# Attention and two feed-forward blocks on one core: queries in two buffers, a first load in two parts, the gate's row on another queue, and a new order of attention's steps

## The chip, the cores and the metric

The kernel runs on one core of one Trainium2 chip. The metric is the time of one execution on the device, in microseconds (us). The engines are TensorE (PE: matmuls, and PEld: the weight loads for them), VectorE (DVE), ScalarE (ACT), GpSimd (POOL) and SyncE (SP, which here only issues DMAs). Each engine works through its own queue in order, and waits on semaphores for the others.

## The reference

Attention is computed for 4 batches of 8 heads, 576 tokens and 64 columns a head: a causal softmax and, beside it, a read from a memory matrix, mixed by a gate for each head. Two feed-forward blocks follow on all 2304 tokens.

```python
scores = q @ k.T / 8;  causal mask;  a = softmax(scores)
local = a @ v
q_p = where(q > 0, q, exp(q) - 1) + 1
mem_out = (q_p @ M_prev) / (q_p . z_prev + 1e-6)
g = 1 / (1 + exp(-beta))                      # one for each head
x = g * mem_out + (1 - g) * local             # then to (2304, 512)
h = x @ w_in;  x = max(0.01 * h, h) @ w_out   # 512 -> 2048 -> 512
out = ((x @ w_a) * (x @ w_b)) @ w_o2          # 512 -> 1536 -> 512
```

## The kernel before

Attention works on 16 pairs of heads, w = 0 to 15. For a pair, `load_qk` brings keys and queries with the head's columns on partitions into one of three buffers (`raw0` to `raw2`). `scores` multiplies them on PE in row tiles of 128 tokens, tile i being (i + 1) * 128 columns wide (the causal part); `scores_tail` does the last 64 rows of two pairs at once. `least` (line 566, or 596 for the tail) is a DVE instruction that adds the mask, writes the scores to SBUF and takes their extreme; `exp_of` (line 513) is the exponential on ACT with its sum; `recip` (lines 524 and 528, DVE) inverts the sums; `norm` (line 540, on DVE or POOL) multiplies a row tile by its inverse sum and by 1 - gate. These instructions are 128, 256, 384, 512 or (tail) 576 columns wide, one for each head and row tile: 144 `norm` steps in all. `probs_T` transposes the result on PE (line 617) and ACT or DVE copies it out of PSUM (lines 331, 333); `pv_local` (line 696) and `pv_memory` (line 668) are the matmuls with v and with the memory, and `store` copies their sum out.

Beside that, two pairs at a time share a load of 128 x 1536 queries (`load_quad`, u = 0 to 7, 768 KB, tile `qraw`), from which `phi` makes q_p: `low` (line 433, a clamp), `exp` (436, ACT), `high` (439), `times` (444 and 449: q_p times z_prev, written back into `qraw`), `total` (454, a sum over the columns) and `scale` (338). There is a single `qraw` tile, so a load can start only after `total` of the load before has read it.

`gates_of_heads` loads the 8 values of beta to all partitions (tile `bt`, on SP's queue behind two larger loads), and makes `gate`, `keep` (1 - gate), `keept` and `gateq` from it in a handful of small DVE instructions.

The order of all 1206 steps, and the engine that each runs on, is written out in `ORDER`: a letter for the engine (A ACT, D DVE, E PE, G POOL, S SP) and the step's number. Each engine issues its steps in that order. A cost table inside `Plan` (`timed`) is used in the kernel only to decide how many filling matmuls (`spin`, line 308, whose result nothing reads) PE runs while it waits at the start. Behind attention, in the same order, come 48 matmuls of the first feed-forward block (`first`), and four halves of a weight block are prepared on DVE, ACT and POOL (`weight`, lines 197 to 226). Then the two feed-forward blocks run, which the change does not touch: three matmuls for each product (lines 284 to 286).

Of the kernel before, what the change touches and what calls it, by code (L numbers as in the profile page):

```python
# [11 lines left out]
F32 = mybir.dt.float32  # L12
# [9 lines left out]
P = 128  # L22
# [8 lines left out]
def chunks(pr):  # L31
# [9 lines left out]

TURN = {"row": 97.0, "full": 152.0, "col": 152.0, "quad": 152.0}
# [73 lines left out]
def attention_moe_moe2(ctx: ExitStack, tc, kqT, qn, vn, m_prev, beta, w_in, w_out, w_a, w_b, w_o2, out):  # L116
# [172 lines left out]
    def attention(att, plan):  # L289
# [66 lines left out]
        def gates_of_heads():  # L356
# [5 lines left out]
            def left(_):  # L362
                nc.vector.tensor_scalar(keep, gate, -1.0, 1.0, ALU.mult, ALU.add)
                for j, r in enumerate(rows_):
                    nc.vector.tensor_copy(keept[r], keep[r, j:H:2])
# [814 lines left out]
```

## Time and profile before

| | |
|---|---|
| median of 3 runs | 1049.55 us (1049.55 to 1050.54) |
| the profiled execution | 1049.57 us |
| its span in the trace | 1047.4 us |
| first scores of attention start | 4.66 us into the span |
| first feed-forward matmul starts | 192.57 us |
| last matmul of attention | 214.4 us |

The profile shows one execution. Its span runs from the first to the last instruction; the 2.2 us between span and time lie around it. A window of the trace gives, for each engine, the time that it was busy, PE's granted clock (1.00 is full speed, 0.5 half of it) and the load of the DMA engines. A group of instructions has its source line, engine, operation, tiles and shape, their count, busy time and mean duration, and the idle time in front of them with what ended it. The chain of waits is followed back from the last instruction: at each step to what released it.

### The profile page before, as it was taken

How to read it: one execution, taken by the hardware profiler on the slowest of the kernel's cores; microseconds unless marked ns; L12 is line 12 of the kernel's file. 1: busy time of each engine (PE TensorE's matmuls, PEld its weight loads, DVE VectorE, ACT ScalarE, POOL GpSimd, SP SyncE). 2: the span in 40 equal slices, each digit the busy share in tenths (PEclk: the TensorE clock that was granted, in tenths of full speed). 3: DMA queues.
4: the chain of work that ended last, by engine and by line, in shares of the span. 5: the costliest groups of instructions: out<-in, count | busy, mean ns of one | idle time of the engine just before them, and what ended most of it. 6: DMA issues, size and time to landing. Idle time of an engine off the chain costs nothing.

```text
span 1047.4 us, 14319 instructions
## 1 busy us (share of the span) xinstructions
PE 1031.7 (98%) x5423; PEld 830.0 (79%) x5425; DVE 714.7 (68%) x1436; ACT 391.1 (37%) x905; POOL 326.1 (31%) x273
## 2 busy tenths in 40 slices
PE   9889999999999999999999999999999999999998
PEld 4556666788888888888888887888888888888887
DVE  7889999877575757484846593772973964955324
ACT  6888888665323222222223342322112121211110
POOL 4346434025434434243434131330330420511000
PEclk9999999999999999999999999999999999999999
DMA  6233432211111111010111010110110210200022
GB/s 219 89 110 116 146 119 79 73 55 67 61 41 61 61 41 57 24 61 24 57 41 61 1 52 29 61 61 1 61 61 1 81 41 7 89 26 1 1 81 100
DMA packets 19061, 63.31 MB, mean 60 GB/s; under 512 B 2352, under 2 KB 2352, under 8 KB 18992
## 3 DMA queue, kind: packets, MB, share of 16 engines
q1 hardware_dynamic: 18992, 62.40, 17.4%
q8 instruction: 42, 0.69, 0.3%
q14 instruction: 27, 0.22, 0.1%
HBM read 57.68 MB, written 4.72 MB: 60 GB/s over the span
## 4 chain that ended last, share of the span: by engine, by line
PE 82%; DVE 12%; ACT 2%; DMA 2%; issue 1%; SPq 0%; DVEq 0%; ACTq 0%
PE b L284 26%; PE b L285 26%; PE b L286 26%; DVE p L540 3%; DVE p L566 2%; PE b L696 1%; DMA qraw<-in_qn 1%; PE b L617 1%; ACT p L513 1%; PE b L558 1%; DVE phi L439 1%; DVE xh L937 1%; DMA bt<-in_beta 1%; DVE nr L454 1%; DVE phi L433 1%
## 5 line engine op out<-in xcount | busy, mean ns | idle before, releaser
L284 PE MATMUL b<-xh,w 128*128 128x512 f32 (+1 forms) x800 | 295.2, 369 | 0.0
L285 PE MATMUL b<-xh,w 128*128 128x512 f32 (+1 forms) x800 | 294.5, 368 | 0.0
L286 PE MATMUL b<-xh,w 128*128 128x512 f32 (+1 forms) x800 | 294.3, 368 | 0.0
L223 POOL TENSOR_TENSOR wa<-wa,w 128x512 f32<-128x512 f32 x64 | 108.7, 1699 | 507.4 <-DVE wh L217 384.8
L284 PEld LDWEIGHTS b<-xh,w 128*128 128x128 f32 x800 | 150.8, 189 | 25.4
L286 PEld LDWEIGHTS b<-xh,w 128*128 128x128 f32 x800 | 150.8, 188 | 25.1
L285 PEld LDWEIGHTS b<-xh,w 128*128 128x128 f32 x800 | 150.9, 189 | 24.9
L212 ACT CAST w<-wa 128x512 fp32r<-128x512 f32 x67 | 41.6, 621 | 227.3 <-DVE wa L204 225.4
L1041 DVE TENSOR_TENSOR gf<-b,gf 128x512 f32<-128x512 f32 (+1 forms) x60 | 38.2, 636 | 125.0 <-PE b L286 125.0
L944 DVE TENSOR_TENSOR hl<-gf,hl 128x512 fp32r<-128x512 f32 (+1 forms) x66 | 50.1, 759 | 77.7 <-ACT hl L943 77.3
L1007 DVE TENSOR_TENSOR xf<-b,xf 128x512 f32<-128x512 f32 (+1 forms) x140 | 87.0, 634 | 19.1 <-PE b L286 17.1
L226 POOL TENSOR_TENSOR w<-wa,wr 128x512 fp32r<-128x512 f32 x65 | 90.0, 1385 | 20.8 <-DVE wr L220 15.8
L943 ACT CAST hl<-gf 128x512 fp32r<-128x512 f32 (+1 forms) x91 | 52.5, 577 | 91.4 <-DVE gf L1041 89.9
L984 ACT ACTIVATE gf<-b 128x512 f32<-128x512 f32 (+1 forms) x76 | 42.0, 553 | 108.3 <-PE b L286 108.3
L284 PE MATMUL b<-hl,w 128*128 128x512 f32 (+1 forms) x220 | 81.1, 369 | 0.0
L285 PE MATMUL b<-hl,w 128*128 128x512 f32 (+1 forms) x220 | 81.0, 368 | 0.0
L286 PE MATMUL b<-hl,w 128*128 128x512 f32 (+1 forms) x220 | 80.9, 368 | 0.0
L1039 ACT COPY gf<-b 128x512 f32<-128x512 f32 (+1 forms) x60 | 32.6, 543 | 115.8 <-PE b L286 114.9
L513 ACT ACTIVATE p<-p,stat 128x384 f32<-128x384 f32 (+3 forms) x128 | 71.2, 563 | 7.9 <-DVE stat L566 7.7
L1060 DVE TENSOR_TENSOR xf<-b,xf 128x512 f32<-128x512 f32 x90 | 60.6, 685 | 19.1 <-PE b L286 18.7
L197 DVE TENSOR_SCALAR wh<-wraw 128x512 uint32<-128x512 uint32 x68 | 64.8, 952 | 1.1 <-DMA wraw<-in_w_out 1.1
L566 DVE CUSTOM_DVE_ANT_0 p<-b,mask 128x384 f32<-128x384 f32 (+3 forms) x128 | 56.1, 480 | 8.6 <-PE b L558 8.2
(120 smaller groups left out, 1752.3 us busy)
## 6 DMA issues: line engine op xcount, KB each, us to landing
wraw<-in_w_in SPq DMA_DIRECT2D x16, 512.0 KB, 3.4
wraw<-in_w_out SPq DMA_DIRECT2D x16, 512.0 KB, 3.4
qraw<-in_qn SPq DMA_DIRECT2D x8, 768.0 KB, 4.9
wraw<-in_w_a SPq DMA_DIRECT2D x12, 512.0 KB, 3.2
wraw<-in_w_b SPq DMA_DIRECT2D x12, 512.0 KB, 3.2
wraw<-in_w_o SPq DMA_DIRECT2D x12, 512.0 KB, 3.2
vs<-in_vn SPq DMA_DIRECT2D x16, 320.0 KB, 3.0
raw<-in_kqT SPq DMA_DIRECT2D x8, 576.0 KB, 3.7
```

The source lines that it names most:

```text
L197: nc.vector.tensor_scalar(u("h"), self.raw[i][:, :, 1], 0x7FFFFFFF, None, ALU.bitwise_and)
L223: (nc.gpsimd if eng == "POOL" else nc.vector).tensor_tensor(t["a"], t["a"], f32(half(0)), ALU.subtract)
L226: (nc.gpsimd if eng == "POOL" else nc.vector).tensor_tensor(half(1), t["a"], t["r"], ALU.add)
L284: nc.tensor.matmul(outp, l_hi, r_hi, start=start, stop=False)
L285: nc.tensor.matmul(outp, l_hi, r_lo, start=False, stop=False)
L286: nc.tensor.matmul(outp, l_lo, r_hi, start=False, stop=stop)
L513: nc.scalar.activation(t, t, AF.Exp, bias=s[:, 0, col : col + 1], scale=-1.0, accum_out=s[:, 1, col : col + 1])
L566: nc.vector.tensor_tensor_reduce(one(p, [P, wd]), plan.tiles[banks[j]][:, c : c + wd], mask[:, off : off + wd], -0.125, BIG, ALU.add, ALU. ...
L943: after(1, lambda: nc.scalar.copy(t[:, 0, c], gf))
L944: after(1 if eng is nc.vector else 2, lambda: eng.tensor_tensor(t[:, 1, c], gf, f32(t)[:, 0, c], ALU.subtract))
L1007: nc.vector.tensor_tensor(y[pr][:, dm, c], op[:, 0:n], y[pr][:, dm, c], ALU.add)
L1060: nc.vector.tensor_tensor(y[:, i], op, y[:, i], ALU.add)
```

## The change

- **Queries in two places.** `qraw` becomes two buffers, `qraws[0]` (the old place) and `qraws[1]` (on the memory of the tile `hl0`, which is used only when the feed-forward block starts). Load u goes to buffer u % 2.
- **The first pair in two parts.** `load_first` brings the first 256 of pair 0's 576 columns and then the other 320. The first `scores` step becomes row tiles 1 and 0 in place of 2 and 0, which needs only the first part.
- **The gate's row.** `bt` is loaded from ACT's queue, as the first thing there. `keep` is made on POOL, and `gateq` by three copies in place of six.
- **The loads' order.** SP's queue begins raw0 (two parts), raw1, queries 0, raw2, queries 1, v0, m0, v1; before, it was raw0, queries 0, beta, raw1, raw2, v0, m0, v1.
- **A new `ORDER`.** The steps on each engine come in another order, and some on another engine. From the first use of the queries counted back to their load, the list had 27 to 38 steps between the two for loads 1 to 7; it has 87 to 141 now. Counts of the steps that can run on more than one engine, by the letters of the two lists:

| step (columns) | before | after |
|---|---|---|
| `norm` 128 | DVE 23, POOL 9 | POOL 32 |
| `norm` 256 | DVE 25, POOL 7 | DVE 12, POOL 20 |
| `norm` 384 | DVE 22, POOL 10 | POOL 32 |
| `norm` 512 | DVE 22, POOL 10 | DVE 24, POOL 8 |
| `norm` 576 | DVE 4, POOL 12 | DVE 7, POOL 9 |
| `low` 512 | DVE 8 | DVE 6, POOL 2 |
| `times` 512 | DVE 4, POOL 4 | DVE 3, POOL 5 |
| `times` 640 | DVE 5, POOL 3 | DVE 7, POOL 1 |
| `scale` 512 | DVE 2, POOL 6 | DVE 4, POOL 4 |
| `scale` 640 | DVE 3, POOL 5 | DVE 4, POOL 4 |
| copies out of PSUM | ACT 171, DVE 21 | ACT 173, DVE 19 |
| a cast and a sum in `weight`, a cast in `first` (4 each) | DVE 8, others 4 | DVE 3, others 9 |

- In the cost table a DMA's rate becomes 220 (150 for a split load) in place of 360 bytes per ns; it changes only the count of filling matmuls.

```diff
 ORDER = (
-    'S0 S7 S1 S8 S11 S9 S10 E27 S113 E36 D28 D34 A29 D39 D12 A2 D32 A13 D30 A35 D3 D37 E41 A40 D14 A31 D4 D15 A38 '
-    'D17 A33 D42 A18 D44 A43 D19 A45 E46 D5 D20 S70 D57 D61 D58 D53 D59 G60 D62 D54 D47 G56 D50 E89 G55 D16 A90 '
+    'S0 A2 D3 S1 D6 S7 G4 D5 S8 S11 S71 E27 S9 S10 D34 S113 D30 A35 E36 D28 A31 D32 A29 E41 D37 D39 A38 D42 A33 '
+    'A40 D44 A43 D57 D53 D54 D58 G55 A45 E46 G59 D61 G60 D62 D47 S70 G56 E89 D50 G65 E87 A90 D48 E114 G66 D51 A49 '
+    'D88 G64 E123 A52 D67 D12 G63 D119 A13 D68 D117 G69 A120 D115 E91 A118 D124 E93 D14 A92 A116 E95 D15 A125 D17 '
...
+        t = main.tile([P, 2 * WIDE], F32, tag="hl0", bufs=1, name="qraw1")
+        qraws = [att.tile([P, 1536], F32, name="qraw0"), t[:, 0:1536]]
...
+            def plus(_):
+                nc.vector.tensor_scalar(bt, bt, 1.0, None, ALU.add)
+                nc.vector.reciprocal(gate, bt)
...
+            nc.scalar.dma_start(bt, beta.unsqueeze(0).to_broadcast([P, H]))
             nc.scalar.activation(gateq[:, 0, 0:2], ident[:, 0:2], AF.Exp)
...
-            dma(lambda _: nc.sync.dma_start(bt, beta.unsqueeze(0).to_broadcast([P, H])), 4096, w=["bt"], at=-150)
...
+        def load_first():
+            c = FIRST
+            rest = lambda _: nc.sync.dma_start(raws[0][:, :, c:S], kqT[0][:, :, c:S])
+            dma(lambda _: nc.sync.dma_start(raws[0][:, :, 0:c], kqT[0][:, :, 0:c]), P * 2 * c * 4, w=["raw0.0"], at=-160)
+            dma(rest, P * 2 * (S - c) * 4, w=["raw0.1"], at=-159)
 
         def load_quad(u):
             def go(_):
-                t = one("qraw", [P, 1536])
-                nc.sync.dma_start(t, qn[u // 2, u % 2])
-
-            dma(go, P * 1536 * 4, w=["qraw0", "qraw1"], at=u * 200 - 120 if u else -140, behind=[f"raw{2 * u % 3}"])
+                nc.sync.dma_start(qraws[u % 2], qn[u // 2, u % 2])
+
+            dma(go, P * 1536 * 4, w=[f"qraw{u % 2}.{x}" for x in range(2)], at=u * 200 - 120 if u else -140, behind=[f"raw{2 * u % 3 if u else 1}.1"])
...
-        load_qk(0)
+        load_first()
         gates_of_heads()
+        load_qk(1)
         load_quad(0)
-        load_qk(1)
...
-            for x, tiles in enumerate(((2, 0), (1,), (3,))):
+            for x, tiles in enumerate(((2, 0), (1,), (3,)) if w else ((1, 0), (2,), (3,))):
```

## Rows read from the trace of the kernel before

**Rows 1.** The page's first line: the span of the profiled execution.

```profile
span 1047.4 us, 14319 instructions
```

**Rows 2.** Windows: stretch, length, each engine's busy time (instructions), PE's clock, DMA.

```profile
core 0: us, PE busy (x) PEld busy (x) DVE busy (x) ACT busy (x) POOL busy (x), PEclk, DMA share, GB/s
...
4.66:192.50 187.84, 179.05 (x1316) 114.80 (x1318) 173.37 (x594) 156.06 (x473) 78.15 (x91) 0.98 0.39 122
...
40.00:50.00 10.00, 8.04 (x46) 5.22 (x46) 6.42 (x28) 8.20 (x27) 3.24 (x4) 0.83 0.22 77
...
60.00:70.00 10.00, 7.89 (x65) 5.47 (x63) 7.87 (x33) 6.42 (x20) 6.91 (x8) 1.00 0.52 165
...
130.00:140.00 10.00, 8.09 (x50) 4.87 (x47) 9.75 (x32) 6.21 (x20) 7.10 (x9) 0.94 0.48 156
140.00:150.00 10.00, 10.00 (x71) 6.49 (x71) 9.10 (x31) 9.08 (x30) 0.00 (x0) 0.89 0.23 76
...
220.00:230.00 10.00, 10.00 (x46) 8.29 (x45) 9.66 (x16) 7.67 (x17) 3.07 (x3) 1.00 0.15 52
```

**Rows 3.** The chain of waits between 0 and 100 us, shares by what it ran through.

```profile
by line: DMA qraw<-in_qn 14.3%; DVE p L566 11.9%; DVE p L540 9.4%; DMA bt<-in_beta 6.7%; ACT p L513 6.7%; PE b L696 6.5%; PE b L617 5.7%; DVE phi L439 4.9%; PE b L558 4.0%; DVE phi L433 3.9%; DVE nr L454 3.3%; DVE qraw L444 3.3%; issue 2.5%
```

**Rows 4.** The tile qraw until 200 us: shortest, median, longest ns; idle until its DMA.

```profile
L433 DVE TENSOR_SCALAR phi<-qraw x16: 407/481/1476, 7.4 to 163.2; 128x512 f32<-128x512 f32 x8, 128x640 f32<-128x640 f32 x8
...
L444 DVE TENSOR_TENSOR qraw<-phi,qraw x9: 676/691/692, 9.9 to 149.4; 128x512 f32<-128x512 f32 x9
...
  DMA qraw<-in_qn: 5.3, 2
...
DMA to landing us min/median/max: 4.0/4.9/8.1
```

**Rows 5.** Timeline of the first 20 us: start, length, engine, line, what [idle before].

```profile
0.73 0.39 SPq L390 DMA_DIRECT2D raw<-in_kqT  x1
...
4.66 2.02 PE L558 MATMUL b<-raw 64*128 64x384 f32 x12
...
6.40 0.56 DVE L566 CUSTOM_DVE_ANT_0 p<-b,mask 128x384 f32<-128x384 f32 x1 [6.40 <-PE b L558]
...
8.40 0.21 ACT L374 ACTIVATE bt<-bt 128x8 f32<-128x8 f32 x1 [0.69 <-DMA bt<-in_beta]
...
14.25 0.22 DVE L524 TENSOR_REDUCE stat<-stat 128x2 f32<-128x4 f32 x2
...
15.44 0.43 PE L617 MATMUL b<-ident,p 128*128 128x128 f32 x2
```

**Rows 6.** Groups until 195 us, shapes apart: the filling matmuls (count, busy us, mean ns).

```profile
L308 PE MATMUL b<-mask 128*128 128x512 bf16 x39 | 10.7, 425 | 1.7 <-POOL mask L292 1.6 <-issue 0.2
```

**Rows 7.** Groups until 195 us, shapes apart: norm on DVE and on POOL.

```profile
L540 DVE TENSOR_SCALAR p<-p,stat,keep 128x384 f32<-128x384 f32 x20 | 12.2, 620 | 0.0
...
L540 DVE TENSOR_SCALAR p<-p,stat,keep 128x512 f32<-128x512 f32 x20 | 11.1, 557 | 0.0
...
L540 POOL TENSOR_SCALAR p<-p,stat,keep 128x512 f32<-128x512 f32 x10 | 9.7, 971 | 7.7 <-ACT phi L436 7.7
...
L540 DVE TENSOR_SCALAR p<-p,stat,keep 128x256 f32<-128x256 f32 x23 | 9.5, 429 | 0.3
...
L540 POOL TENSOR_SCALAR p<-p,stat,keep 128x384 f32<-128x384 f32 x10 | 7.1, 709 | 0.0
...
L540 DVE TENSOR_SCALAR p<-p,stat,keep 128x128 f32<-128x128 f32 x21 | 7.6, 367 | 0.1
...
L540 POOL TENSOR_SCALAR p<-p,stat,keep 128x256 f32<-128x256 f32 x7 | 4.9, 704 | 17.3 <-DVE stat L524 11.2 <-DVE stat L528 3.5 <-PE b L586 1.7
...
L540 POOL TENSOR_SCALAR p<-p,stat,keep 128x128 f32<-128x128 f32 x9 | 4.6, 510 | 13.9 <-DVE stat L528 10.1 <-PE b L490 3.8
```

**Rows 8.** The chain of waits between 100 and 195 us, one piece: eight norms in a row.

```profile
145.67 2.94 DVE p L540 x8
```

**Rows 9.** Timeline at 163 us: a POOL instruction and a DVE instruction that overlap.

```profile
163.31 1.45 POOL L444 TENSOR_TENSOR qraw<-phi,qraw 128x512 f32<-128x512 f32 x1 [0.62 <-DVE phi L439]
...
163.56 1.89 DVE L338 TENSOR_TENSOR phi<-phi,nr 128x640 f32<-128x640 f32 x1
```

More of the change, by code (lines that the diff above doesn't have):

```diff
@@ L359, in gates_of_heads @@
             rows_ = [slice(j * 64, j * 64 + 64) for j in range(2)]
-            nc.scalar.activation(gateq[:, 0, 0:2], ident[:, 0:2], AF.Exp)
[L362 to L365, printed above, removed]
-            def spread(_):
-                for kt in range(4):
-                    nc.vector.tensor_copy(gateq[:, :, kt * 4 : kt * 4 + 4], g)
-                for j, r in enumerate(rows_):
-                    nc.vector.tensor_copy(gateq[r, :, 16:18], g[r, :, j * 2 : j * 2 + 2])
@@ L373, in gates_of_heads @@
-            dma(lambda _: nc.sync.dma_start(bt, beta.unsqueeze(0).to_broadcast([P, H])), 4096, w=["bt"], at=-150)
-            add(lambda _: nc.scalar.activation(bt, bt, AF.Exp, scale=-1.0), {"ACT": 100}, r=["bt"], w=["bt"], at=-20)
-            add(lambda _: nc.vector.tensor_scalar(bt, bt, 1.0, None, ALU.add), {"DVE": 72}, r=["bt"], w=["bt"], at=-20)
-            add(lambda _: nc.vector.reciprocal(gate, bt), {"DVE": 120}, r=["bt"], w=["gate"], at=-20)
-            add(left, {"DVE": 590}, r=["gate"], w=["keep"], at=-19)
@@ L378, in gates_of_heads, with left, tails_, spread @@
-            add(spread, {"DVE": 1265}, r=["gate"], w=["gateq"], at=60)
+            def plus(_):
+                nc.vector.tensor_scalar(bt, bt, 1.0, None, ALU.add)
+                nc.vector.reciprocal(gate, bt)
+            def left(eng):
+                ENG[eng].tensor_scalar(keep, gate, -1.0, 1.0, ALU.mult, ALU.add)
+            def tails_(eng):
+                for j, r in enumerate(rows_):
+                    copy(eng, keept[r], keep[r, j:H:2])
+            def spread(eng):
+                copy(
+                    eng, gateq[:, :, 0:16].rearrange("p u (k f) -> p u k f", k=4),
+                    g.unsqueeze(2).to_broadcast([P, 2, 4, 4]),
+                )
+                for j, r in enumerate(rows_):
+                    copy(eng, gateq[r, :, 16:18], g[r, :, j * 2 : j * 2 + 2])
@@ new lines, in gates_of_heads @@
+            nc.scalar.dma_start(bt, beta.unsqueeze(0).to_broadcast([P, H]))
+            nc.scalar.activation(gateq[:, 0, 0:2], ident[:, 0:2], AF.Exp)
+            add(lambda _: nc.scalar.activation(bt, bt, AF.Exp, scale=-1.0), {"ACT": 115}, w=["bt"], at=-20)
+            add(plus, {"DVE": 160}, r=["bt"], w=["gate"], at=-20)
+            add(left, {"DVE": 170, "POOL": 330}, r=["gate"], w=["keep"], at=-19, port=True)
+            add(tails_, {"DVE": 400, "POOL": 660}, r=["keep"], w=["keept"], at=-19, port=True)
@@ L380, in rows @@
+            add(spread, {"DVE": 650, "POOL": 1000}, r=["gate"], w=["gateq"], at=60, port=True)
         def rows(w, j):
@@ L540, in go @@
                 ENG[eng].tensor_scalar(live[p], live[p], stats[w % 3][:, 3, col : col + 1], k, ALU.mult, ALU.mult)
-            add(go, c_ts(n), r=[f"{st}.r{col}", "keep"], w=[p], at=at, port=True)
+            add(go, c_ts(n), r=[f"{st}.r{col}", "keept" if key == "t" else "keep"], w=[p], at=at, port=True)
         def scores(w, tiles, at):
-            st, raw = f"stat{w % 3}", f"raw{w % 3}"
+            st = f"stat{w % 3}"
+            raw = [f"raw{w % 3}.{x}" for x in range(1 if max(tiles) < 2 else 2)]
             banks = [plan.ring("sc") for _ in range(2)]
@@ L586, in go @@
                             nc.tensor.matmul(t[j * 64 : j * 64 + 64, 0:288], x[:, 1, 512:S], x[:, 0, c], start=True, stop=True)
-            add(go, {"PE": 968}, r=[f"raw{v % 3}" for v in pairs_], w=sum(banks, []), at=at, mode="quad")
+            add(go, {"PE": 968}, r=[f"raw{v % 3}.{x}" for v in pairs_ for x in range(2)], w=sum(banks, []), at=at, mode="quad")
             for n, v in enumerate(pairs_):
@@ L913, in timed @@
                 if e == "SP":
-                    wire = max(wire, start[i] + cost[e] / count + 650.0) + size / 360.0
-                    done[i] = wire + 800.0
+                    wire = max(wire, start[i] + cost[e] / count + 650.0) + size / (220.0 if count == 1 else 150.0)
+                    done[i] = wire + 900.0
             return on, start
```

24 lines of the change are left out of this document (13 added, 11 removed), and 111 rows, old and new, of the table ORDER.

## The prediction, before the changed kernel ran

> **What bounds the kernel now.** I read the windows first. From about 192 us on, PE is busy all the time, 10.00 of 10 us at full clock, with DVE at 9.66 and not in its way [rows 2]; the change leaves that work alone, so the end of the kernel moves by as much as attention's end moves. In the 187.84 us from the first scores to the first feed-forward matmul, DVE is busy 173.37, ACT 156.06, POOL 78.15 and PE 179.05 [rows 2]. PE's figure flatters it: the 39 filling matmuls, 10.7 us [rows 6], are in it. The chain of waits runs through DVE's `least` and `norm`, and for 14.3% of its first 100 us through the load of the queries, 6.7% through beta's row [rows 3]. So attention is limited by DVE, with holes where the single `qraw` tile makes everybody wait for a DMA.
>
> What PE could gain at most, I count in PE's own time: 187.84 - 179.05 = 8.8 us idle; filling behind the first scores, 32 of 39 (seven run before them), 32/39 x 10.7 = 8.8; and slow clock, 0.17 x 10 us at 40, 0.06 x 10 at 130 and 0.11 x 10 at 140, together 3.4, each time after PE had waited [rows 2, 6]. That is 21 us, and 4.66 us before the first scores [rows 5]. No part of the change can gain more than lies here.
>
> **The change part by part.**
>
> *First pair in two parts.* The load is issued at 0.73 us and PE starts at 4.66, 3.9 us later [rows 5]. The first part has 256 of 576 columns. The bounds are no gain and the left-out share of 3.9 us, 0.56 x 3.9 = 2.2. A 768 KB load lands in 4.0 us at best [rows 4], hardly later than this 576 KB one, so bytes are little of it: I take -0.7. The second part is needed only one scores step later.
>
> *Gate's row and the front.* Today DVE does its first `least` at 6.40 us, its first inverse sum only at 14.25, and PE its first transpose at 15.44 [rows 5]. In between DVE runs the first half of `phi` on queries 0: two clamps at 0.48 and two products at 0.69 [rows 4], and two sums (line 439) that I price like the products: 3.7 us. In the new order these come behind the norms of pair 0, and queries 0 load behind raw1. The transposes can start up to 3.7 us sooner, in time that PE now fills [rows 6]. The work isn't gone: DVE has it to do later, where it is no longer alone on the path. Against it: the first three steps on DVE now wait for beta's exponential. Today that runs at 8.40 us [rows 5], and no consumer was urgent. From ACT's queue nothing stands in front of the row, but if it landed as late again, DVE's `least` could begin at some 9.3 us (8.40, 0.2 for the exponential, seven small instructions) in place of 6.40, that is +2.9. The other bound is -3.7. I take -2.5, nearer the low end, since a row of 8 values issued first should land by the time of the first scores.
>
> The Trainium skill, page "DMA: Bandwidth & Descriptors", section "Issuing engines are not separate DMA queues", speaks against this: DMAs of all issuing engines run on the same 16 DMA engines and interleave, and issuing from another one saves only the sequencer's time. By that rule the row would still share the engines with the first load, and the sum would end 5.4 us later; no row here shows a load from ACT's queue.
>
> *Queries in two places.* DVE stands idle 5.3 us in two waits for `qraw`, with landings up to 8.1 us [rows 4]; the two windows where that happens show PE idle 1.96 and 2.11 us, and the first also a clock of 0.83, which costs 1.7 [rows 2]. Together 5.8. With two buffers and the loads some 100 steps ahead in place of 33, at 1206 steps in about 210 us some 17 us ahead, a landing of 8.1 us is covered. What could be late next is the keys' load, whose place in the order stays. Some of that idle time has other causes: I take -5.0, between -3.4 and -5.8.
>
> *DVE's load.* From DVE to POOL go net 23 norms of 128 columns, 13 of 256 and 22 of 384; two of 512 and three of 576 go back. By the rows' means DVE sheds 23 x 0.367 + 13 x 0.429 + 22 x 0.620 = 27.7, less 5 x 0.557 = 2.8 (the tail's three at the price of 512): 24.9 us. By the chain, where eight norms pass in 2.94 us [rows 8], it is 53 x 0.37 = 19.5; the means hold waits. POOL takes 23 x 0.510 + 13 x 0.704 + 22 x 0.709 = 36.5, less 5 x 0.971 = 4.9: +31.6 [rows 7], so about 110 of 188 us. The moves inside `phi` nearly cancel; five weight and copy steps leave DVE as well, at 0.5 to 0.7 each some 3 us. DVE falls from 173 to about 150, ACT stays near 158, and is then the fullest beside PE. What that gives PE: the window at 130 and the next, where DVE was at 9.75 with the weights' steps in the middle of attention, hold 1.91 us idle and 1.7 of clock; of these 3.6 I take -2.0 (bounds 0 and -3.6). Of the idle time left, 8.8 - 1.96 - 2.11 - 1.91 = 2.8, I take -1.0, with new waits of up to +4 on the other side, since a row of the old order says nothing of where the new one makes an engine wait.
>
> *The rest.* `keep` and the gate's copies, fewer and partly on POOL, are hidden under the first load's landing; without that cover they cost the seven small instructions named above, and these stand in the bound of +2.9.
>
> **Sum.** -0.7 - 2.5 - 5.0 - 2.0 - 1.0 = -11.2 us. The profiled execution took 1049.57 us, its span 1047.4 [rows 1], and the median of the runs is 1049.55, so 1038.4 for either.
>
> **The rivals.**
>
> *All of it comes.* The front gains both bounds that its parts allow (-2.2 and -3.7), and -5.8, -3.6, -2.8 follow: -18.1, 1031.5. For it: DVE with 23 us less is no longer the limit anywhere. Against: in the new order ACT and PE are both full, and two engines that are full in order rarely meet without gaps.
>
> *Only the data waits go.* DVE's relief is eaten by waits among four engines of similar load; what remains is -0.7 - 5.0 = -5.7: 1043.9.
>
> *Beta's row comes late.* +2.9 in place of -2.5: 1043.8. For it: 6.7% of the chain ran through this row [rows 3], and DVE now stands behind it. Against: then two larger loads were in front.
>
> *The second buffer doesn't load sooner* (the change doesn't do what it says): SP issues in order, and a query load behind a blocked keys load would wait with it. Then the third term is gone: 1043.4. Against it, the loads' places in the list.
>
> *Slower: POOL and DVE keep each other out.* At 163.31 us a POOL instruction runs 1.45 us; a DVE product begun inside it takes 1.89 us, just until 0.69 us after POOL's end [rows 9], 0.69 being what such an instruction takes by itself [rows 4]; and norms of 384 columns take 0.620 on DVE while those of 512 take 0.557 [rows 7]. So these instructions exclude each other. A norm moved to POOL then holds the pair of engines longer than on DVE: 31.6 - 24.9 = +6.7 us in all. If the shared time, not DVE's, is the limit, all of that lands on the end, and the waits of DVE's 43 remaining norms for a POOL instruction of 0.7, half of it on average, if a quarter of them meet one (an estimate), add 43 x 0.35 / 4 = 3.8. With -2.5, -5.0 and -0.7 kept, +10.5 - 8.2 = +2.3: 1051.9. It decides from the point where POOL's 110 us and DVE's instructions that need the same access fill the 188. Against: POOL is busy only 78 of 188 us today and 110 by the sum [rows 2], which leaves room, if the order puts DVE's other work beside it.
>
> The Trainium skill states the same as a rule, on the page "SBUF — State Buffer", section "Who interferes with whom": the port pair shared by DVE and GpSimd is an exclusive lock for a whole instruction. The trace agrees (1.89 us for a 0.69 us instruction); by the rule in its strict form this rival is the one to fear.
>
> **How the numbers follow.** My forecast, a few us around 1038.4, has 0.50; all of it 0.14; only the data waits 0.13; beta late 0.07; the buffer not sooner 0.05; slower 0.11. The range reaches from 1030 to 1047, which leaves out the slower case and the tails of the others. About 0.2%, 2.1 us, is what a measurement of this kernel can tell from no change. Faster by more than that: 0.86, as all cases but the last lie below 1047.4; within it 0.04, from the tail of the mild cases and the front of the slower one; slower 0.10.
>
> **What would show it.** Right: no idle time until the DMA of `qraw`, the clock at 1.00 in every window, first transposes before 12 us, DVE at about 150 us and POOL at 110 before the first feed-forward matmul, which starts at some 181 us. Wrong: ACT's first exponential of beta later than the first scores' end; DVE norms and products far longer than their shortest; POOL as the last of the waits in front of transposes; a new hole where ACT's copies are late.

## The result, and the profile after

The changed kernel takes 1039.43 us (median; 1037.55 to 1039.65) where the kernel before, beside it, takes 1049.55: a ratio of 0.9902, 95% interval 0.9883 to 0.9922, so 8 to 12 us less. The prediction was 1038.4. The profiled execution took 1037.55 us, with a span of 1035.8. One execution in what follows, the profiled one of a_norms (1276.57 us at a mean granted clock of 0.753), was in a slower state of the chip and is left out, with its trace.

Windows of the kernel after, with the columns of [rows 2]; the first goes from the first scores to about the first feed-forward matmul (179.05 us, 192.57 before), the second to attention's last matmul:

```profile
4.88:181.00 176.12, 172.05 (x1306) 110.60 (x1307) 164.82 (x544) 157.35 (x476) 108.69 (x137) 1.00 0.42 132
4.88:202.90 198.02, 193.95 (x1449) 127.16 (x1449) 175.86 (x566) 169.30 (x500) 112.02 (x142) 1.00 0.39 123
20.00:30.00 10.00, 9.33 (x67) 5.69 (x67) 9.86 (x32) 7.87 (x27) 3.23 (x6) 1.00 0.61 197
30.00:40.00 10.00, 8.19 (x64) 5.78 (x63) 9.90 (x31) 8.37 (x24) 5.86 (x9) 1.00 0.25 59
40.00:50.00 10.00, 10.00 (x76) 6.03 (x74) 9.71 (x39) 9.86 (x33) 8.70 (x11) 1.00 0.50 173
60.00:70.00 10.00, 9.96 (x71) 6.68 (x73) 9.12 (x37) 9.90 (x32) 8.62 (x10) 1.00 0.40 151
130.00:140.00 10.00, 10.00 (x77) 6.33 (x76) 9.93 (x30) 8.94 (x32) 8.45 (x10) 1.00 0.63 225
140.00:150.00 10.00, 10.00 (x89) 6.78 (x88) 9.48 (x33) 9.11 (x27) 5.60 (x8) 1.00 0.34 94
```

Against [rows 2]: the clock is 1.00 in every window of 10 us. The windows at 40, 60 and 130, in which PE stood idle for 1.96, 2.11 and 1.91 us, are full. There is a new hole of 1.81 us at 30. POOL's busy time rose from 78 to 109 us as forecast, but DVE's fell only from 173 to 165, not to 150.

The chain of waits, by line, from 0 to 100 us:

```profile
by line: DVE p L586 12.8%; PE b L578 12.3%; PE b L637 9.7%; PE b L716 8.6%; ACT p L532 6.5%; DVE phi L458 5.2%; DVE qraw L463 5.0%; DMA raw<-in_kqT 4.9%; DVE pt L616 4.3%; DVE nr L473 4.2%; PE b L688 3.1%; DVE pt L559 3.0%; DVE p L559 2.3%;
```

In [rows 3] the first entries were the load of the queries, DVE and the load of beta. Now neither load is in it, and PE's scores, transposes and products with v (L578, L637, L716) have 30.6% together. Of the chain over the whole span, on the page of the profile, PE has 90% (82% before) and DVE 7% (12%):

```profile
PE 90%; DVE 7%; ACT 2%; DMA 0%; issue 0%; POOL 0%; SPq 0%; DVEq 0%; ACTq 0%; POOLq 0%
```

The timeline of the first 13 us (start, length, engine, line, what, [idle before]), to set beside [rows 5]:

```profile
3.51 0.21 ACT L387 ACTIVATE bt<-bt 128x8 f32<-128x8 f32 x1 [0.88 <-DMA bt<-in_beta]
...
4.88 0.92 PE L578 MATMUL b<-raw 64*128 64x256 f32 x8 [0.58 <-DMA raw<-in_kqT]
...
6.40 1.83 PE L578 MATMUL b<-raw 64*128 64x384 f32 x8 [0.28 <-DMA raw<-in_kqT]
...
9.53 0.22 DVE L543 TENSOR_REDUCE stat<-stat 128x2 f32<-128x4 f32 x2
...
12.00 0.82 PE L637 MATMUL b<-ident,p 128*128 128x128 f32 x6
```

The exponential of beta comes at 3.51 us (8.40 before), the first inverse sum at 9.53 (14.25) and the first transposes at 12.00 (15.44). The first scores, which have only the first part of the load to wait for, start at 4.88, no earlier than before (4.66).

The tile `qraw` until 200 us (shortest, median, longest ns), for [rows 4]; among what its engines waited for, the load of the queries is gone, though the median landing is later:

```profile
L463 DVE TENSOR_TENSOR qraw<-phi,qraw x10: 691/694/1510, 17.0 to 170.9; 128x512 f32<-128x512 f32 x10
...
DMA to landing us min/median/max: 5.1/5.9/9.6
```

### Where the 11.7 us are

The last matmul of attention ended at 214.6 us before and ends at 202.9 now, 11.7 sooner; the feed-forward blocks behind it take the same time, so this is the whole change. Two accounts show where it comes from. The first counts what PE does beside its own work, up to that last matmul:

| | before | after | gain |
|---|---|---|---|
| until the first scores | 4.66 | 4.88 | -0.2 |
| filling matmuls behind the first scores (32 and 24) | 7.6 | 6.2 | 1.4 |
| idle, 20 to 40 us | 1.2 | 2.5 | -1.3 |
| idle and slow clock, 40 to 70 us | 6.3 | 0.5 | 5.8 |
| idle and slow clock, 130 to 150 us | 3.7 | 0.0 | 3.7 |
| idle elsewhere | 1.2 | 1.1 | 0.1 |

That is 9.5 us; the other 2.2 lie in PE's own matmuls, which have less busy time in the windows though they are the same ones, and I can't put them to a cause. (Slow clock is length x (1 - clock): 30 x 0.06 for 40 to 70 us, and 20 x 0.09 for 130 to 150.)

The second account takes the start of the last matmuls with v of each pair of heads (the group `tail,vs` of the timeline) as milestones, in us:

| kernel | pair 0 | 1 | 2 | 3 | 8 | 9 | 15 |
|---|---|---|---|---|---|---|---|
| before | 28.1 | 51.8 | 62.4 | 76.5 | 131.1 | 147.9 | 214.4 |
| after | 24.6 | 46.4 | 58.2 | 70.6 | 125.5 | 136.1 | 202.7 |
| sooner by | 3.6 | 5.4 | 4.2 | 5.8 | 5.7 | 11.8 | 11.7 |

So the lead is built in two places: 5.4 us in the first two pairs, and 6.1 us between the ends of pairs 8 and 9, which took 16.8 us before and take 10.7 now. The two accounts agree on the second place in kind, not in size, and they differ on the holes between 40 and 70 us. That difference is what the experiments had to settle: are the parts' prices their own, or does one hole only hand its time to the next?

### The profile page after: what moved, and what is told of

Its sections match the earlier page's. It is cut to its first block, busy times and chain, and to the rows that moved or that the text cites. A ratio compares the mean times of both kernels' runs of the same rounds, so it can differ in the third digit from the quotient of the medians.

```text
span 1035.8 us, 14320 instructions
## 1 busy us (share of the span) xinstructions
PE 1024.1 (99%) x5414; PEld 825.3 (80%) x5414; DVE 701.3 (68%) x1376; ACT 394.2 (38%) x910; POOL 359.8 (35%) x325
## 4 chain that ended last, share of the span: by engine, by line
PE 90%; DVE 7%; ACT 2%; DMA 0%; issue 0%; POOL 0%; SPq 0%; DVEq 0%; ACTq 0%; POOLq 0%
PE b L286 26%; PE b L287 26%; PE b L288 26%; PE b L716 3%; PE b L637 3%; PE b L578 3%; DVE p L586 1%; PE b L688 1%; ACT p L532 1%; PE b L509 1%; DVE xh L957 1%; DVE phi L458 1%; DVE qraw L463 0%; DMA raw<-in_kqT 0%; PE b L606 0%
## 5 line engine op out<-in xcount | busy, mean ns | idle before, releaser
L287 PEld LDWEIGHTS b<-xh,w 128*128 128x128 f32 x800 | 150.9, 189 | 24.9
L559 POOL TENSOR_SCALAR p<-p,stat,keep 128x384 f32<-128x384 f32 (+3 forms) x92 | 61.3, 680 | 46.3 <-DVE stat L547 22.6
```

The costliest lines, as they stand in the source:

```text
L287: nc.tensor.matmul(outp, l_hi, r_lo, start=False, stop=False)
L559: ENG[eng].tensor_scalar(live[p], live[p], stats[w % 3][:, 3, col : col + 1], k, ALU.mult, ALU.mult)
```

## The experiments

Ratios are to the kernel before, run beside each, with 95% intervals; 0.1% is 1.05 us. The kernel after stands at 0.9902, known to 0.2%, so that differences to it below some 2 us say little.

### Parts of the change put into the kernel before

**b_two: the second place of the queries alone.** The loads are moved up to where both buffers allow it.

```diff
-                t = one("qraw", [P, 1536])
-                nc.sync.dma_start(t, qn[u // 2, u % 2])
+                nc.sync.dma_start(qraws[u % 2], qn[u // 2, u % 2])
...
+ORDER = behind(ORDER, [("S71", "S70"), ("S214", "S290"), ("S358", "S289"), ("S501", "S433"), ("S645", "S576"), ("S793", "S743"), ("S942", "S866")])
```

> The kernel before with one part of the change alone: the second place for the queries, and each later load of queries moved up in SP's order to stand right behind the nearest earlier load of keys or of the memory. Everything else, the engines of all steps included, is as before. The theory (each wait for the queries costs what the windows at 40 and 60 us show, 5.0 us with its slow clock): about 1044.5 us, no idle time of DVE until the queries' DMA, the clock at 1.00 at 40 us. The rival (DVE's load sets the pace, so the holes are filled by work that comes late anyhow): 1047 to 1049.

Measured: 1048.11 us, ratio 0.9989 (0.9976 to 1.0002): a gain of 1.2 us, which may be none. Its windows:

```profile
40.00:50.00 10.00, 10.00 (x76) 6.42 (x76) 9.65 (x37) 10.00 (x33) 4.99 (x6) 1.00 0.44 152
50.00:60.00 10.00, 7.96 (x53) 5.02 (x51) 9.72 (x22) 6.42 (x21) 3.57 (x4) 0.83 0.13 39
60.00:70.00 10.00, 10.00 (x78) 6.60 (x74) 9.21 (x31) 8.56 (x26) 6.27 (x8) 1.00 0.36 85
130.00:140.00 10.00, 8.09 (x36) 4.71 (x34) 9.45 (x26) 6.09 (x20) 4.39 (x4) 0.79 0.28 86
140.00:150.00 10.00, 10.00 (x71) 6.64 (x68) 8.20 (x28) 8.53 (x27) 0.00 (x0) 0.87 0.31 113
```

The holes at 40 and 60 us are closed, and one of 2.04 us with a clock of 0.83 has opened at 50, where DVE is at 9.72 of 10. That hole need not be the second place's doing: b_place below has it too, with one place for the queries. The hole at 130 is still there. By the milestones this kernel is 2.7 us ahead of before at pair 8 and 1.1 at pair 9: the place behind pair 8 takes more than half of the lead back. PE idles as long there as before (1.91 us), but the lower clock costs it 3.4 us in place of 1.7. This fits a DVE that sets the pace, so that a wait for the queries that is taken away comes back as a wait for DVE; a part of it comes back as slow clock.

**b_norms: the norms alone on the engines of after.** 68 norms go to POOL and 15 to DVE, each at its old place in the order.

```diff
+ORDER = on(on(ORDER, "G", TO_POOL), "D", TO_DVE)
```

> The kernel before with only the engines of the norms taken from the changed kernel: 68 norms from DVE to POOL, 15 from POOL to DVE, each at its old place in the order. The theory (DVE's load limits PE between the holes; the prediction put 3 us on it): about 1046.5 us, POOL's busy time in attention about 30 us up, DVE's 13 down. The rival (POOL and DVE keep each other out, or POOL is late at places that were ordered for DVE): 1049 to 1053.

Measured: 1051.78 us, ratio 1.0020 (1.0005 to 1.0036), 2 us slower. In the view of the tile `qraw`, what DVE waited for:

```profile
  DMA qraw<-in_qn: 8.0, 4
```

[Rows 4] had 5.3 us in 2 such waits, and b_place below has 5.5 in 4, so it is the idle time that grew and not the number alone. This is one trace, of the second slowest of the twelve executions (1054.06 us). That a DVE with less to do meets the late loads sooner would explain it, but is not shown to be the cause of the loss; POOL's norms coming late at places that were ordered for DVE, which was also expected, costs PE 1.4 us of idle time in the same trace.

**b_two_norms: both.**

> The kernel before with both of these parts: two places for the queries with the loads moved up, and the norms' engines of the changed kernel. The theory of parts that add: 1049.5 - 5.0 - 3.0 = 1041.5 us. If the one only opens the way for the other, less than either sum would give: below 1041. If the order of the other steps is what makes norms on POOL pay, no better than the two places alone, 1044.5 or above.

Measured: 1046.82 us, ratio 0.9981 (0.9970 to 0.9992), a gain of 2.0 us, where the parts alone gave 1.2 and -2.1. So together they are worth 2.9 more than their sum, known to some 2, and still 8 short of the change.

**b_place: three steps of the place at 132 us.** The weight step `join` moves up to the end of `shift`, its cast goes to ACT, and one norm to POOL, as in the new order.

```diff
+ORDER = behind(ORDER, [("D746", "D745"), ("D747", "A771")])
+ORDER = on(on(ORDER, "A", {747}), "G", {785})
```

> The kernel before with three steps of one place as the new order has them: the weight step `join` directly behind `shift`, its cast on ScalarE instead of VectorE, and one norm of 384 columns on POOL. In the trace of before, VectorE runs these three (0.67, 0.81 and 1.19 us) at 132.6 to 135.1 us, while the `least` steps of the tenth pair's scores stand behind them and TensorE waits 1.91 us for these. Theory, the place is what its list says: VectorE comes to this `least` 2.7 us sooner, TensorE loses no time there, and with the clock that it then keeps the whole kernel is 2.7 to 3.6 us faster (1046 to 1047, beside 1049.55). Rival, the place only shows a VectorE that is late anyway: a hole of the same size opens a little later, and the kernel is 0 to 0.7 us faster.

Measured: 1047.92 us, ratio 0.9993 (0.9976 to 1.0009), so no gain that this comparison can tell from none. Its timeline on DVE:

```profile
133.93 0.45 DVE L447 TENSOR_SCALAR phi<-qraw 128x512 f32<-128x512 f32 x1 [0.70 <-DMA qraw<-in_qn]
134.30 0.55 DVE L580 CUSTOM_DVE_ANT_0 p<-b,mask 128x384 f32<-128x384 f32 x1
```

In its trace the theory holds in the place itself: `least` comes at 134.30 in place of 136.49 us (the clamp, which before took 1.48 beside a POOL instruction, is at 0.45), and pairs 8 to 9 take 13.4 us in place of 16.8. But DVE now waits 0.70 us for the queries, which it hadn't done there, and between pairs 10 and 11 another 1.1 us are lost; at pair 15 a lead of 2.2 us is left in the trace, and by the ratio 0.7. The place gives what the theory said. In the trace the next waits take about a third of it; by the ratio, known to 1.7 us, little is left, as the rival said.

This kernel shows one thing more. Up to pair 8 it is the kernel before, step for step, and yet pair 1 ended at 48.2 us, not 51.8, while pair 2 ended at 62.2 (62.4). A hole that a single trace shows at 40 us is in another execution at 50:

```profile
50.00:60.00 10.00, 8.02 (x49) 4.99 (x51) 9.72 (x25) 6.41 (x20) 3.57 (x4) 0.83 0.11 28
```

This is b_two's window at 50 over again, without a second place. DVE's wait for the second load of queries was 1.35 us here and 3.44 in the trace of before. So whether the second place or chance brings that load in time, pair 2 ends at 62.0 to 62.4 us; of the two holes in [rows 2], only the one at 60 us went with the second place (8.01 us of PE here, 10.00 in b_two).

### Parts of the change taken out of the kernel after

**a_one: a single place for the queries**, each load behind the last use of the one before it.

```diff
-        qraws = [att.tile([P, 1536], F32, name="qraw0"), t[:, 0:1536]]
+        qraws = [att.tile([P, 1536], F32, name="qraw0")] * 2
+ORDER = behind(ORDER, [("S71", "D21"), ("G72", "D26"), ("S214", "D81"), ("S358", "D224"), ("S501", "D368"), ("S645", "D511"), ("S793", "D655"), ("S942", "D803")])
```

> The changed kernel with a single place for the queries again, each load of them moved back in SP's order to stand right behind the sum that frees the place (and one clamp moved behind its load). The theory (the second place is worth its waits, 5.0 us, more where PE is now the limit and each hole is PE's): 1039.4 + 5 to 8 = 1044.5 to 1047.5 us, with idle time until the queries' DMA back in the trace. The rival (the new order has so much other work ready that the waits are covered): 1039.5 to 1041.

Measured: 1045.85 us, ratio 0.9982 (0.9968 to 0.9996): 8 us of the gain are gone. Its engines waited 13.6 us for the queries, and the window at 30 shows what one load can cost:

```profile
  DMA qraw<-in_qn: 13.6, 5
```

```profile
30.00:40.00 10.00, 5.65 (x26) 4.60 (x30) 4.97 (x12) 7.03 (x22) 6.26 (x7) 0.66 0.00 1
```

More than half of the loss is there, where the second load of queries comes behind the first one's use, which the new order has put off: pairs 0 to 1 take 26.4 us in place of 21.8. It is a price of the front, so I took the question up once more:

**a_late: loads 0 and 1 as they are, loads 2 to 7 in one place.**

```diff
-                nc.sync.dma_start(qraws[u % 2], qn[u // 2, u % 2])
+                nc.sync.dma_start(qraws[u == 1], qn[u // 2, u % 2])
+ORDER = behind(ORDER, [("S358", "D224"), ("S501", "D368"), ("S645", "D511"), ("S793", "D655"), ("S942", "D803")])
```

> The new kernel with query loads 0 and 1 as they are, but loads 2 to 7 all in one place, so that each from load 3 on starts only behind the last use of the load before it. The earlier kernel of this kind with one place for all lost 6.3 us, most of it in the first 40 us. Theory, the second place is worth in the running part what the prediction put on it: 4 to 6 us are lost, 1042 to 1044. Rival, it is worth that only in the first 40 us: a loss of at most 2 us, 1038 to 1040.

Measured: 1043.38 us, ratio 0.9950 (0.9933 to 0.9966), 5.0 us more than after. The wait on DVE in its timeline, and the two windows around it:

```profile
66.24 0.43 DVE L465 TENSOR_SCALAR phi<-qraw 128x512 f32<-128x512 f32 x1 [3.48 <-DMA qraw<-in_qn]
```

```profile
60.00:70.00 10.00, 6.75 (x47) 4.66 (x43) 6.45 (x27) 5.93 (x19) 5.98 (x10) 0.94 0.39 133
70.00:80.00 10.00, 10.00 (x65) 5.54 (x66) 7.38 (x25) 8.66 (x29) 7.76 (x10) 0.89 0.30 92
```

After has 9.96 and 9.88 there at full clock. The trace is that of the slowest of the six executions (1046.46 us). In it, one late load makes PE idle 3.25 us and costs 1.7 of clock, and pairs 2 to 3 take 17.0 us in place of 12.4. In the new order, then, the second place is worth about 5 us in the running part, and in the old one 1.2.

**a_norms: the norms back on the engines of before**, at their new places.

```diff
+ORDER = on(on(ORDER, "D", TO_DVE), "G", TO_POOL)
```

> The changed kernel with the engines of the norms as before: 68 norms back from POOL to DVE, 15 back to POOL, each at its new place in the order. The theory (3 us of the gain come from DVE's relief): about 1042.5 us, DVE some 13 us fuller in attention, POOL 30 us emptier. The rival (DVE's relief is what the whole order rests on, and DVE is the limit again): 1047 to 1050.

Measured: 1046.74 us, ratio 0.9974 (0.9963 to 0.9986), 7.6 us more than after. The same moves that cost the old order 2.1 us are worth 7.6 in the new one. By what waits they are worth it isn't shown, since there is no trace of this kernel to set beside the others.

**a_allpool: all 144 norms on POOL**, 43 more than in after.

```diff
+ORDER = on(ORDER, "G", NORMS)
```

> The changed kernel with all 144 norms on POOL, the 43 that are left on DVE too. This puts some 30 us more on POOL (109 to about 140 of 176) and takes 20 to 25 off DVE. If POOL's and DVE's mutual exclusion is near its limit: 8 us slower or more, 1047 and above, with longer DVE products. If PE is the limit and both have room: within 2 us of 1039.4. If POOL's latency in front of the transposes is what hurts: slower too, but with PE waiting for POOL's norms and DVE's products no longer than now.

Measured: 1045.72 us, ratio 0.9971 (0.9960 to 0.9983), 7.2 us more than after. Its windows:

```profile
4.88:181.00 176.12, 167.46 (x1250) 106.72 (x1252) 144.85 (x485) 151.71 (x456) 129.81 (x174) 0.98 0.42 130
110.00:124.00 14.00, 11.06 (x71) 6.88 (x70) 10.58 (x38) 11.26 (x37) 6.53 (x10) 0.88 0.45 149
```

DVE has 20 us less to do than in after and POOL has 130 of 176, so neither is full; still PE idles 4.6 us more. What PE waited for, in the same stretch (us, times, longest):

```profile
PE b L657 <- POOL p L579: 4.1, 7, 1.4
PE b L598 <- DVE stat L606: 2.9, 1, 2.9
```

The first line, where after has one wait of 0.2 us, is transposes that wait for POOL's norms. The second is the hole at 110 us, the largest, with a clock of 0.88; pairs 6 to 7 take 16.4 us there in place of 11.7. The timeline of it, POOL's rows, DVE's and then PE's:

```profile
107.88 0.22 POOL L508 TENSOR_TENSOR nr<-nr,gateq 128x18 f32<-128x18 f32 x1
108.08 0.56 POOL L360 TENSOR_SCALAR xh<-xf 128x448 fp32r<-128x448 f32 x1
108.61 1.25 POOL L363 TENSOR_TENSOR phi<-phi,nr 128x640 f32<-128x640 f32 x1
109.82 1.12 POOL L363 TENSOR_TENSOR xh<-xf,xh 128x448 fp32r<-128x448 f32 x1
116.94 0.91 POOL L579 TENSOR_SCALAR pt<-pt,stat,keept 128x576 f32<-128x576 f32 x1 [6.00 <-DVE stat L567]
```

```profile
108.13 3.36 DVE L363 TENSOR_TENSOR phi<-phi,nr 128x512 f32<-128x512 f32 x1 [1.56 <-POOL nr L508]
111.42 0.28 DVE L606 CUSTOM_DVE_ANT_0 p<-b,mask 128x128 f32<-128x128 f32 x1
```

```profile
112.92 1.13 PE L598 MATMUL b<-raw 64*128 64x512 f32 x4 [2.89 <-DVE stat L606]
```

POOL's four instructions run one behind the other until 110.9 us. DVE's product, begun at 108.13, lasts until 111.49 and takes 3.36 us (two of its kind and size take 1.42 together in the trace of after, at 23.04 us), so by the times it stood behind the one that was running and the two that began after it. Behind it stands `least`, for which PE waits 2.89 us and POOL's next norm 6.0. This is the exclusion of [rows 9], with a price: not the half of one instruction that the prediction's rival put on a meeting, but the whole row of POOL's instructions. It is not the whole loss, since the waits for POOL's norms are the longer sum; the product itself began late, too, 1.56 us behind a step of POOL. DVE's load by itself explains nothing here: there is less of it, and the time is longer.

**a_whole: the first pair loaded whole.**

```diff
-            rest = lambda _: nc.sync.dma_start(raws[0][:, :, c:S], kqT[0][:, :, c:S])
-            dma(lambda _: nc.sync.dma_start(raws[0][:, :, 0:c], kqT[0][:, :, 0:c]), P * 2 * c * 4, w=["raw0.0"], at=-160)
+            rest = lambda _: None
+            dma(lambda _: nc.sync.dma_start(raws[0], kqT[0]), P * 2 * c * 4, w=["raw0.0"], at=-160)
```

> The changed kernel with the first pair of heads loaded whole, by one DMA, and nothing in the place of the second part. The prediction took 0.7 us for the two parts; the trace of the changed kernel shows its first scores at 4.88 us, 0.22 later than before, and the second scores waiting for the other part until 6.40. The theory now (the parts gain nothing): 1038.5 to 1039.5 us, first scores at about 4.7. If the parts are worth what was predicted: 1040.1.

Measured: 1040.67 us, ratio 0.9929 (0.9915 to 0.9942), 2.8 us more than after. The first scores, and a window behind them:

```profile
6.33 0.92 PE L578 MATMUL b<-raw 64*128 64x256 f32 x8 [2.03 <-DMA raw<-in_kqT]
```

```profile
8.50:12.00 3.50, 2.98 (x8) 0.79 (x7) 2.29 (x11) 2.98 (x12) 0.00 (x0) 0.50 0.99 399
```

PE waits 2.03 us for the load, starts 1.45 later than in after, and runs at a clock of 0.50 soon behind that wait (1.2 GHz of 2.4). The gate's row is late as well, though ACT issues it at 0.72 us as in after:

```profile
6.59 0.21 ACT L387 ACTIVATE bt<-bt 128x8 f32<-128x8 f32 x1 [3.94 <-DMA bt<-in_beta]
```

DVE's first `least` stands behind it, at 8.08 us in place of 5.84. So this run prices two delays at once, that of the scores and that of the row. In the kernel before, the whole load was there in time for scores at 4.66 us, with no row beside it and the queries behind it on the queue; here the row is beside it and the second pair's keys are behind it. Which of the two slows it was not tried by itself; the next run bears on it.

**a_beta: the gate's row on SP's queue, behind both parts of the first load.** In the order, the second part moves in front of the exponential.

```diff
-            nc.scalar.dma_start(bt, beta.unsqueeze(0).to_broadcast([P, H]))
...
+                nc.sync.dma_start(raws[0][:, :, c:S], kqT[0][:, :, c:S])
+                nc.sync.dma_start(bt, beta.unsqueeze(0).to_broadcast([P, H]))
```

> The changed kernel with beta's row on SP's queue, issued behind the first pair's two parts. The theory (a row behind those loads lands after them, and DVE's first steps stand behind it): ACT's exponential of it at 6 to 7 us in place of 3.51, DVE's first extreme at 7.5 to 8 in place of 5.84, and the time 1 to 2 us up, about 1041. The rival (in the front nothing is tight, since the exponentials of pair 0 limit it): below 1040.

Measured: 1040.18 us, ratio 0.9919 (0.9906 to 0.9932), 1.8 us more than after, within what after itself is uncertain by. Its timeline:

```profile
2.10 0.59 SPq L416 DMA_DIRECT2D bt<-in_beta  x1
...
4.22 1.65 PE L582 MATMUL b<-raw 64*128 64x256 f32 x8
...
6.26 0.21 ACT L387 ACTIVATE bt<-bt 128x8 f32<-128x8 f32 x1 [4.04 <-DMA bt<-in_beta]
```

The exponential comes at 6.26 in place of 3.51 us, so the row does come sooner by its own queue. But the first scores start at 4.22 us here, sooner than in after (4.88) and in before (4.66). The first part of the load, in the DMA issues of a_beta and then of after (KB, us to landing):

```profile
raw<-in_kqT SPq DMA_DIRECT2D x1, 256.0 KB, 3.2
```

```profile
raw<-in_kqT SPq DMA_DIRECT2D x1, 256.0 KB, 4.1
```

Both are issued at 0.72 us. What differs is the row, which ACT issues at the same time in after, and the second pair's keys, issued at 2.73 in place of 2.08 us. So the row very likely slows the load beside it; a_whole points the same way. The two effects nearly cancel in the first scores, which end at 5.87 us here and at 5.80 in after. Behind them the late row shows: the first `least` comes at 7.76 in place of 5.84 us and the first transposes at 14.7 in place of 12.00. How much of that lasts to the end, the ratio can't tell from nothing.

### The new order up to a point, then the old one

Both kernels are the code of after; from the named pair on, the remaining steps follow in the order, and on the engines, of before.

**a_front: new order for pair 0 only.** Its query loads from 2 on are issued as late as before.

> The code of the new kernel, with its order of steps up to the end of the first pair of heads and from there on the remaining steps in the order, and on the engines, of the kernel before (so the query loads 2 to 7 are issued as late as before). Theory, the front's gain lasts: the first pair ended 3.6 us sooner in the new kernel, so 1045.5 to 1046.5. Rival, the next wait takes it: the work on the first queries was put off, the holes of the query loads and of the place at 130 us remain, and 1048 to 1050 comes out.

Measured: 1048.27 us, ratio 0.9987 (0.9975 to 0.9999), a gain of 1.4. By its milestones it is 1.4 us ahead of before at pair 0, at 62.7 us 0.3 behind it at pair 2, and 1.4 ahead at the end. The rival is nearer: the next hole takes the lead, and some of it returns at the place behind pair 8.

**a_eight: new order up to the end of pair 8.**

> The code of the new kernel, with its order of steps up to the end of the ninth pair of heads (125.5 us in its trace) and from there on the remaining steps in the order, and on the engines, of the kernel before. Theory, the place behind it is worth 6.1 us (the tenth pair took 16.8 us before and 10.7 after): attention ends at 125.5 + 83.2 = 208.7 in place of 202.7 us, and the kernel takes 1043 to 1044. Rival, that place was long only because VectorE came to it late: with the first nine pairs in the new order it is short in the old order too, and 1038 to 1040 comes out.

Measured: 1043.28 us, ratio 0.9944 (0.9933 to 0.9956), 4.4 us more than after, as the theory had it. Its windows:

```profile
130.00:140.00 10.00, 9.08 (x59) 5.74 (x59) 9.95 (x38) 8.30 (x27) 2.51 (x3) 1.00 0.21 70
140.00:150.00 10.00, 10.00 (x88) 6.58 (x86) 9.91 (x25) 9.59 (x31) 0.41 (x1) 1.00 0.48 148
```

DVE is at 9.95 and 9.91 of 10, POOL is nearly unused, and pairs 8 to 9 take 14.4 us (10.7 in after, 16.8 in before). So the old order is slow in this place even when it is reached with all that the new order brings; 2.4 of the 6.1 us, though, were a debt that came from before it.

Its start shows something that the comparison with after must know. The first scores:

```profile
4.84 1.65 PE L576 MATMUL b<-raw 64*128 64x256 f32 x8 [0.54 <-DMA raw<-in_kqT]
...
6.96 3.36 PE L576 MATMUL b<-raw 64*128 64x384 f32 x8
```

The same matmuls (four of 256 columns and four of 128, then four of 384 and four of 512) took 0.92 and 1.83 us in the trace of after. Pair 0 ends at 26.6 us here, as in the traces of a_late (26.6), a_one (26.4) and a_front (26.7), and not at 24.6; in a_allpool it ends at 24.7, with first scores of 0.92 us. But for a_one, whose second load of queries is later, all six have the same steps up to there. So 2.0 us of after's front belong to the execution and not to the steps: two of six traces have them, and of the 3.6 us of lead at pair 0 only 1.5 are there in the other four. After's profiled execution was also the fastest of its kernel, 1037.55 beside 1039.38 to 1039.65; these 1.9 us fit, but the others have no trace.

## Why the prediction was right, point by point

The time came out as forecast, 1039.43 for 1038.4, and as faster. The sum of -11.2 stands against -11.7 in the traces and -10.1 in the medians. Its terms did less well.

*What bounds the kernel.* Right. PE, with some 21 us to gain at most, was the thing to count; the gain is half of that, and 9.5 of the 11.7 us were idle time, clock and filling as counted. Most signs named for it came too: clock 1.00, first feed-forward matmul at 179 us (181 forecast), POOL at 109 us (110), ACT at 157 (158). DVE's 150 did not: it was 165. And one sign named for a wrong prediction came, DVE norms and products far longer than their shortest.

*First pair in two parts, -0.7.* It did not come as such. The first scores came no sooner than before, 4.88 against 4.66 us, so against the kernel before it gave nothing. The step that failed is that this part and the gate's row were priced apart: the prediction asked what the load does to the row, and not what the row does to the load. With the row elsewhere (a_beta) the first part landed in 3.2 us and not in 4.1, and the scores began at 4.22, which is 0.4 sooner than before, where 0.7 was forecast. Taken out of the new order the two parts cost 2.8 us, known to 2 (a_whole), with the scores 1.45 us later and the row late with them; what the order of the loads adds to that stays open.

*Gate's row and the front, -2.5.* The mechanism was right: first transposes at 12.00 us, before the 12 that were named, by 3.4 us; the bound of +2.9 was idle, since the exponential came at 3.51. On SP's queue it came 2.75 us later (a_beta), 1.4 of it by a later issue (2.10 against 0.72 us) and the rest by a longer landing. By the Trainium skill's rule, page "DMA: Bandwidth & Descriptors", section "Issuing engines are not separate DMA queues", another issuing engine would save only the first of these; here it saved both; but the same row from ACT's queue took 5.8 us to land beside a whole first load (a_whole), so the split load is part of it. The size that lasts was smaller: by the ledger 1.4 us of filling less 0.2, and a_front's 1.4 at the end. The error is the step "the transposes can start up to 3.7 us sooner, in time that PE now fills": PE got the time and then stood idle at 20 to 40 us for 1.3 us more. DVE is full there (9.86 and 9.90 of 10 in its windows, 19.0 of 20 before); that the work on the first queries, put off, is what fills it is read from the order and was not tried.

*Queries in two places, -5.0.* Right in the new order: a_late lost 5.0, and the windows from 40 to 70 us gave 5.8. Wrong as a price of its own, as b_two's 1.2 shows. The step that failed is the assumption that the two windows' loss belongs to the load: the same stretch holds a DVE at its limit (9.72 of 10 at 50 us), and when the load comes in time a hole of like size is there in place of the one at 40, with the second place (b_two) as without it (b_place).

*DVE's load, -2.0 and -1.0.* The mechanism is right (the chain went from DVE to PE), the inputs were off. Until attention's last matmul DVE shed 14.7 us (190.5 to 175.9), not 23. The norms' groups, in the same stretch of before and after:

```profile
L540 DVE TENSOR_SCALAR p<-p,stat,keep 128x256 f32<-128x256 f32 (+3 forms) x92 | 39.3, 485 | 0.4
...
L540 DVE TENSOR_SCALAR pt<-pt,stat,keept 128x576 f32<-128x576 f32 x4 | 2.5, 638 | 0.1
```

```profile
L559 DVE TENSOR_SCALAR p<-p,stat,keep 128x512 f32<-128x512 f32 (+1 forms) x36 | 20.4, 578 | 0.5
...
L559 DVE TENSOR_SCALAR pt<-pt,stat,keept 128x576 f32<-128x576 f32 x7 | 6.3, 907 | 0.0
```

They fell from 41.8 to 26.7 us, by 15.1 and not by 24.9. Two things make the difference. One is that means overlap: the 96 norms before, at the means of [rows 7], come to 47.6 us, but the groups are busy for 41.8; the chain's figure, which gave 19.5, was nearer, and the prediction set it aside. The other is that the norms left on DVE got slower, by shape until 195 us:

```profile
L559 DVE TENSOR_SCALAR p<-p,stat,keep 128x512 f32<-128x512 f32 x24 | 15.6, 661 | 0.0
```

661 ns in place of 557, and for the tail's seven 907 in place of 638, which is 4.4 us for these 31; DVE's longest product in `phi` went from 692 to 1510 ns. The exclusion was in the rows, and the prediction used it for a rival only, not for the term. What the place at 130 us gave was under-sized all the same: the forecast took 2.0 from bounds of 0 and 3.6, and the windows gave 3.7, a_eight 4.4. The "rest", -1.0, came out at +1.2 by the ledger (-0.1 and +1.3).

*The rivals.* Beta late, and the buffer that doesn't load sooner: neither (3.51 us; no wait for `qraw` left). Only the data waits: no, for then the place behind pair 8 would have stayed. All of it: no, 15 us of PE's 25 before its work and beside it are still there. POOL and DVE keeping each other out: the mechanism is real and made the norms on DVE longer, but with 43 of them left there it isn't the limit; with none left (a_allpool) it opens a hole, beside 4.1 us of waits for POOL's norms, which is another matter. In the one place seen it decides not from the point where the two engines fill the stretch, as the rival had it, but where several of POOL's instructions stand in a row beside a DVE step that PE waits for. (The product of [rows 9] has 640 columns, and one such took 0.82 us by itself in the trace of before; the 0.69 set beside it is the time at 512. The reading stands.)

*The sum.* It was right partly by luck. The terms are not each part's own price: put into the old kernel, the second place, the norms, the front and the place at 132 us gave 1.2, -2.1, 1.4 and 0.7 us, 1.2 in all; taken out of the new one, places, norms and the second half of the order cost 5.0 to 8, 7.6 and 4.4. I take it that sum and result agree because the prediction counted PE's losses stretch by stretch, and the whole change removes 9.5 of the 10.0 us in the stretches at 40 to 70 and 130 to 150 us; it named the wrong owner for some.

What stays open: why PE's own matmuls are 2.2 us shorter, what makes the first scores take nearly twice as long in some executions, and whether the row alone slows the first load.

## What to carry to other kernels

Count the loss at the engine that does the unavoidable work, stretch by stretch, and treat this as the most that a change of the whole can bring; don't hand it out to the parts, since a part alone can lose its gain in the next hole. When a step moves to another engine, price it by what the chain shows, not by means that overlap, and where two engines exclude each other, look at how many of the other's instructions stand in a row. And a hole in one trace has no fixed place: before building on it, see it in a second execution.

## What the runs showed of the hardware that was not expected

An instruction of DVE that needs the access shared with POOL, begun while POOL works, can be held over two POOL instructions that begin only after it (3.36 us for some 0.7, in a_allpool).

The same eight matmuls of the first scores (four of 256 columns, four of 128) took 0.92 us in one execution and 1.65 in others, and the next eight (four of 384, four of 512) took 1.83 and 3.36, at the same place behind the same six filling matmuls, while the granted clock of both stretches reads 1.00. The filling matmuls beside them tell more: the single one behind the first scores took 0.39 us in after and 0.61 in a_eight, and ten in a row took 2.33 and 2.50 us further on, but 3.97 in a_whole, at a granted clock of 0.57 (11.35 to 15.25 us). So PE seems to have run near half of its clock in these scores, which is argued from the durations and not shown. A granted clock of 1.00 does not say that PE ran at its fastest there; the rows' own durations have to be looked at too.

A load of 256 KB landed in 4.1 us with the gate's row of 4 KB issued beside it from another queue, and in 3.2 us without the row; the row itself took 2.8 us to land beside that load and 5.8 beside one of 576 KB. The second pair's keys were issued 0.65 us later without the row, so the two are not fully apart; but a small load on another queue looks far from free for the load that it runs beside.
